# A fused attention, expert and feed-forward kernel: twelve decoding steps change place, and so do the loads of q, k and v

## The chip, the core and the metric

The kernel runs on one core of a Trainium2 chip, as one launch. The metric is the device time of that launch in microseconds; a smaller number is better. Engines are called PE or TensorE (matrix multiply), DVE or VectorE, ACT or ScalarE, POOL or GpSimd, and SP or SyncE, which here only issues DMAs. Every engine works through its own queue in order. Data of the inputs and of intermediate tensors in main memory reach the core's memory by DMA, most of them issued from SP's queue.

## The reference, cut to what matters

```python
def reference(**kwargs):          # q, k, v: 4 batches, 8 heads, 576 positions, 64 wide
    attn_out = _attn_ref(q, k, v) # scores * D, D[i, j] = gamma_h ** (i - j) for i >= j, else 0; times v
    x = attn_out.transpose(0, 2, 1, 3).reshape(B * S, H * D)     # 2304 x 512
    x = _moe_ref(x, ...)          # cosine router, each row to 1 of 8 experts:
                                  # gate * (relu(x @ w1[e]) @ w2[e]), w1 512 x 1024
    return _moe2_ref(x, ...)      # h = x @ w_in; (elu(h)) @ w_out, w_in 512 x 2048
```

## The kernel before, in words

The kernel goes through three stages: attention with the router (line 698 on), the eight experts (line 1247 on), and the last feed-forward part (line 1444 on).

**Attention** is a retention: the decay splits into a factor of the query and one of the key, so that earlier positions can be carried in a small state. It runs over ten units (`UNITS`, line 32). Eight units hold 256 positions of one batch, all heads; two (units 4 and 9) hold the last 64 positions of two batches. In its turn a unit u does, in the order in which the instructions are emitted, and so in the order of each engine's queue:

- `scale(u + 2)` on GpSimd: a copy of q (L289) and a product of k with its decay (L282), each for one tile of a later unit
- `carried(u)`: matmuls of q with the state (L359), then `scores(u, 1)`: matmuls (L334), and a mask on VectorE (L339)
- `transposes(u + 1, 0)`: the scaled q and k of the next unit are transposed on TensorE (L309) and copied out by ScalarE (L317)
- the rows of x of an earlier tile (`xrows`, L427 on TensorE, L439 on VectorE, a store from SP at L448), and `pump`, which emits router steps, small instructions of VectorE, until one needs another engine
- `summed(u + 1)`: the state of the next unit, matmuls of scaled k with v (L396), then additions on VectorE (L403 to L409)
- `transposes(u + 1, 1)`, `values(u)`: matmuls of the masked scores with v (L372), copied out by ScalarE (L378), then `scores(u + 1, 0)`, `xrows`, a second `pump`, and tables for the router on GpSimd (`slots`, L591 to L594)

Between these stand the loads (L261, L264) that SP issues. `load(u, which, behind)` names a unit, one or more of q, k and v, and, where given, a copy of ScalarE that SP waits for before it issues the load. q and k have three buffers, v has four.

**Decoding.** The weights of the last part come as 64-bit numbers. Before they can be used they are turned into 32-bit ones and written to main memory (`wd`), in 32 tiles of 128 x 512. A tile takes four steps (`decode_steps`, line 143), one VectorE instruction each (L151, L153, L156, L159); the second also has a Square on ScalarE (L154), and the fourth issues two DMAs on SP: the load of the tile after next (L137 or L140, 512 KB; there are two buffers) and the store of the finished tile (L161, 256 KB). `decode(n)` emits n steps. `NDECA` (line 698) gives attention units 2 to 6 twelve steps between them, one or two in each `pump`. `decode_load(0)` and `(1)` in unit 1 bring the first two tiles.

**The experts** run through 64 iterations i, eight for each expert: `mm1` (L230, into `h`), then `mm2` of the iteration before (L992 and L994, into `acc`). ScalarE makes hh, the high part of the result of `mm1` (L978), VectorE makes hl, its low part (L979). In each iteration one weight tile is loaded (512 KB) and split into a high part (L199, ScalarE) and a low part (L204, VectorE): w1 in even iterations (ra to ha, la), w2 in odd ones (rb to hb, lb). After the split `decode(2)` emits two steps of decoding (line 1301), through iteration 53. Iterations 9 to 21 also build index tables (`compact`, `compact_part`) on VectorE and GpSimd (L1041). The low part of w2 and hl are read by the matmuls of `mm2`.

The names `u`, `i`, `scale`, `summed`, `load` and `decode` below are these.

Of the kernel before, what the change touches and what calls it, by code (L numbers as in the profile page):

```python
# [14 lines left out]
ALU = mybir.AluOpType  # L15
AX = mybir.AxisListType

P = 128
# [21 lines left out]
NU = len(UNITS)  # L40
# [44 lines left out]
def tile_kernel(ctx: ExitStack, tc: tile.TileContext, q, k, v, emb, tau, w1, w2, w_in, w_out, const, out):  # L85
# [165 lines left out]
    def load(u, which="qkv", behind=None):  # L251
        if u >= NU:
            return
        b, c, _ = UNITS[u]
        r = loaded.setdefault(u, {})
        for nm, src in (("q", q), ("k", k), ("v", v)):
            if nm not in which:
                continue
            t = r[nm] = ld.tile([P, H, 2, D], F32, tag="l" + nm, name=f"{nm}{u}", bufs=4 if nm == "v" else 3)
            if c >= 0:  # L260
                ins = [nc.sync.dma_start(out=t.rearrange("p h s d -> p h (s d)"),  # L261
                                         in_=src[b, :, c * 2 * P:(c + 1) * 2 * P, :].rearrange("h (i s) d -> i h (s d)", s=2))]
            else:
                ins = [nc.sync.dma_start(out=t[64 * j:64 * j + 64, :, 0, :], in_=src[b + j, :, 512:576, :].rearrange("h s d -> s h d"))  # L264
                       for j in range(2)]
            if behind is not None:
                after(ins[0], behind)
# [6 lines left out]
    def scale(u):  # L274
        if u >= NU:
            return
        c = UNITS[u][1]
        scaled[u] = {nm: a2.tile([P, 2, H, D], F32, tag=nm + "s", name=f"{nm}s{u}") for nm in "qk"}
        eng = vec if u == 0 else pool

        def decayed(nm, s_, g_):
            eng.tensor_tensor(out=scaled[u][nm][:, s_], in0=loaded[u][nm][:, :, s_, :],  # L282
                              in1=C("g" + nm)[:, g_ * H:(g_ + 1) * H].unsqueeze(2).to_broadcast([P, H, D]), op=ALU.mult)

        m = len(slots_of(u))
        if u == NU - 1:
            decayed("q", 0, 4)
        else:
            eng.tensor_copy(out=scaled[u]["q"][:, :m].rearrange("p s h d -> p h s d"), in_=loaded[u]["q"][:, :, :m, :])  # L289
        if u == 0:  # L290
            meanwhile()
        for s_ in slots_of(u):
            decayed("k", s_, 2 * c + s_ if c >= 0 else 4)
# [401 lines left out]
            if n == g0 + gn - 1:  # L695
                live.append((gi, interleave(*(then(g(gi), gi, p) for g, p in ((expert_steps, (0, 2)), (gate_steps, (2, NPART)))))))

    NDECA = {2: (1, 1), 3: (1, 1), 4: (1, 1), 5: (1, 1), 6: (2, 2)}
    held = None
    for u in range(NU):  # L700
        ns = UNITS[u][2]
        nd = NDECA.get(u, (0, 0))
        before = UNITS[u - 1][2][1] if u and len(UNITS[u - 1][2]) > 1 else None
        if u:
            scale(u + 2)
            load(u + 3, "q")
        carried(u)
        scores(u, 1 if UNITS[u][1] >= 0 else 0)
        transposes(u + 1, 0, "qk" if u else "k")
        if u == 0:  # L710
            load(2, "k", copied[1, 0, "k"])
            scale(2)
            nc.sync.dma_start(out=ct[:, gcols:], in_=const[:, gcols:CSMALL])
            nc.sync.dma_start(out=big[0][:, 2 * P:], in_=const[:, CSMALL + 2 * P:])
            pool.tensor_scalar(out=pre[:, 0, :], in0=C("base"), scalar1=1.0 / P, scalar2=None, op0=ALU.mult)
            pool.tensor_copy(out=lowb, in_=C("lower"))
            pool.tensor_copy(out=parts[:, :, :2], in_=C("id").rearrange("p (n two) -> p n two", two=2))
        if held is not None:
            grouped(held)
        if before is not None:  # L720
            xrows(before)
        if u < NU - 1:
            pump(24, nd[0])
        summed(u + 1)
        if u == 7:
            load_a(0)
            load_b(0)
            load_a(1)
        transposes(u + 1, 1)
        if u == 0:  # L730
            load(3, "q", copied[1, 1, "k"])
        if u:
            load(u + 3, "k", copied.get((u + 1, 1, "k")))
        if u == 1:
            decode_load(0)
            decode_load(1)
        values(u)
        if u == 0:
            load(3, "k", copied[0, "x"])
        load(u + 2, "v", copied[u, "x"])  # L740
        if before is not None:
            grouped(before)
        if u == NU - 1:
            while live:
                pump(100, 0)
        if u + 1 < NU and UNITS[u + 1][1] >= 0:
            scores(u + 1, 0)
        xrows(ns[0])
        held = ns[0]
        if u < NU - 1:  # L750
            pump(24, nd[1])
        for _ in range(6 if u > 6 else 4):
            if ready:
                slots(*ready.pop(0))
# [492 lines left out]
    for i in range(NI1 + 1):  # L1247
# [46 lines left out]
        if i in (IOVER + 6, IOVER + 7):  # L1294
            next(prep)
            next(prep)
        elif IOVER + 8 <= i < IOVER + 15:
            high(0, i - IOVER - 8)
            low_(0, i - IOVER - 8)
        elif i < IOVER + 6 and i != IOVER - 1:  # L1300
            decode(2)
        if i == NI1 - 3:
            Sa(0)
        if i == NI1 - 2:
# [199 lines left out]
```

## Time and profile before

| | us |
|---|---|
| median of 3 runs (750.96 to 752.85) | 751.32 |
| the profiled execution, whole run | 750.73 |
| the profiled execution, its span | 748.9 |
| TensorE busy | 715.6 (96%) |
| VectorE busy | 587.8 (78%) |
| ScalarE busy | 447.0 (60%) |
| GpSimd busy | 240.8 (32%) |
| moved by DMA | 123.79 MB, mean 165 GB/s |

The span goes from the first to the last instruction that the profiler records; the run is somewhat longer. TensorE is the busiest engine, so the first thing to look for is the stretches where it isn't busy or where its granted clock is below 1.00, and what it waits for there. In the rows below a line of the timeline gives the start and the length in us, the engine, the source line, the instruction, output and inputs, how many of them were merged, and in brackets how long the engine had stood idle before and what ended that.

### The profile page before, as it was taken

The page shows a single profiled execution, that of the slowest core. Times are in us where ns is not written, and L with a number is a line of the kernel's source. Part 1 is how long each engine was busy: PE and PEld are TensorE (multiplying, and loading weights), DVE is VectorE, ACT ScalarE, POOL GpSimd, SP SyncE. Part 2 cuts the span into 40 slices and gives each one's busy share as a digit, 9 for nine tenths or more (in the row PEclk, how much of TensorE's full clock was granted, in tenths as well). Part 3 has the DMA queues.
Part 4 walks back from the last instruction along what each step waited for, and adds up shares of the span by engine and source line. Part 5 has one row for each costly group of instructions (what it writes and reads, how often), then busy time and mean ns, then how long its engine had stood idle before and what let it go on. Part 6 is the DMA issues. An engine that isn't in the chain of part 4 may idle for free.

```text
span 748.9 us, 15511 instructions
## 1 busy us (share of the span) xinstructions
PE 715.6 (96%) x5940; PEld 660.0 (88%) x5940; DVE 587.8 (78%) x940; ACT 447.0 (60%) x690; POOL 240.8 (32%) x347
## 2 busy tenths in 40 slices
PE   7987997999999999989999999999999999999996
PEld 6876984899999999989989998988999998999995
DVE  4458587877887899869789889988778998777773
ACT  3343342555655665656676757777566787666562
POOL 3417236216980240100442133244212227311103
PEclk9999897999999999999999999999999999999999
DMA  7768572788789899888424231234222114221002
GB/s 209 221 206 251 156 227 81 220 283 278 266 288 340 275 291 312 299 310 274 142 85 153 71 99 57 84 114 169 84 61 81 57 58 155 75 80 57 28 29 84
DMA packets 101939, 123.79 MB, mean 165 GB/s; under 512 B 12218, under 2 KB 72030, under 8 KB 101862
## 3 DMA queue, kind: packets, MB, share of 16 engines
q1 hardware_dynamic: 97574, 111.71, 47.1%
q0 software_dynamic: 3104, 9.83, 3.7%
q10 hardware_dynamic: 1184, 1.24, 0.5%
q8 instruction: 47, 0.77, 0.4%
q14 instruction: 30, 0.25, 0.1%
HBM read 99.91 MB, written 22.85 MB: 164 GB/s over the span
## 4 chain that ended last, share of the span: by engine, by line
PE 29%; issue 14%; DVE 7%; POOL 4%; ACT 2%; DMA 2%; SPq 0%; POOLq 0%; ACTq 0%; DVEq 0%
PE o L230 12%; PE X L230 7%; PE Y L230 5%; PE h L230 2%; PE acc L992 2%; DMA draw<-in_moe_w_in_dram 1%; POOL out_dram L1416 1%; PE acc L994 1%; POOL qs L1217 1%; POOL qa L1216 1%; DVE hA L1381 1%; POOL qs L1215 1%; DVE glA L1389 1%; DVE xA L1378 1%; POOL qs L1218 1%
## 5 line engine op out<-in xcount | busy, mean ns | idle before, releaser
L1215 POOL TENSOR_TENSOR qs<-qa 128x256 f32<-128x256 f32 x24 | 23.2, 965 | 250.1 <-DMA qa<-wd 49.7
L230 PE MATMUL h<-xth,ha 128*128 128x332 f32 (+7 forms) x252 | 75.1, 314 | 1.2 <-DVEq L1125 1.2
L992 PE MATMUL acc<-hh,hb 128*128 128x342 f32 (+7 forms) x256 | 73.6, 304 | 2.3 <-ACT hh L978 2.3
L992 PE MATMUL acc<-hh,lb 128*128 128x342 f32 (+7 forms) x256 | 73.5, 303 | 0.3 <-DVE lb L204 0.3
L230 PE MATMUL h<-xtl,ha 128*128 128x332 f32 (+7 forms) x252 | 72.9, 305 | 0.0
L978 ACT ACTIVATE hh<-h 128x342 fp32r<-128x342 f32 (+7 forms) x64 | 27.2, 424 | 46.9 <-PE h L230 44.7
L1368 ACT ACTIVATE rA<-hA 128x768 f32<-128x768 f32 x24 | 20.3, 848 | 55.3 <-DVE hA L1361 55.3
L1353 DVE TENSOR_TENSOR u<-Y,m 128x384 f32<-128x384 f32 x48 | 26.6, 554 | 31.8 <-PE Y L230 29.8
L992 PEld LDWEIGHTS acc<-hh,hb 128*128 128x128 f32 x256 | 48.2, 188 | 2.5 <-ACT hh L978 2.5
L230 PEld LDWEIGHTS h<-xth,ha 128*128 128x128 f32 x252 | 48.0, 191 | 1.7 <-DVEq L1125 1.4
L204 DVE TENSOR_TENSOR la<-ra,ha 128x1024 fp32r<-128x1024 f32 x32 | 39.1, 1222 | 12.5 <-ACT ha L199 12.4
L992 PEld LDWEIGHTS acc<-hh,lb 128*128 128x128 f32 x256 | 48.3, 189 | 0.6 <-DVE lb L204 0.6
L230 PEld LDWEIGHTS h<-xtl,ha 128*128 128x128 f32 x252 | 48.1, 191 | 0.0
L204 DVE TENSOR_TENSOR lb<-rb,hb 128x1024 fp32r<-128x1024 f32 x32 | 39.6, 1236 | 9.7 <-ACT hb L199 9.4
L994 PE MATMUL acc<-hl,hb 128*128 128x342 f32 (+7 forms) x256 | 47.0, 305 | 0.0
L230 PE MATMUL h<-xth,la 128*128 128x332 f32 (+7 forms) x252 | 45.7, 303 | 0.0
L917 POOL DMA_INDIRECT row<-xd,idsp x21 | 21.8, 1038 | 71.4 <-ACT xth L958 68.6
L1416 POOL DMA_INDIRECT out_dram<-ob,idc x18 | 20.3, 1128 | 68.4 <-ACT ob L1413 65.9
L339 DVE TENSOR_TENSOR A<-sc,ctbig 128x512 f32<-128x512 f32 (+1 forms) x36 | 22.0, 653 | 22.7 <-PE sc L334 22.7
L994 PEld LDWEIGHTS acc<-hl,hb 128*128 128x128 f32 x256 | 39.0, 189 | 0.6 <-DVE hl L979 0.3
L317 ACT COPY qT<-qTp 128x512 f32<-128x512 f32 x18 | 11.1, 624 | 47.5 <-PE qTp L309 47.5
L230 PEld LDWEIGHTS h<-xth,la 128*128 128x128 f32 x252 | 38.8, 190 | 0.0
(1690 smaller groups left out, 2342.6 us busy)
## 6 DMA issues: line engine op xcount, KB each, us to landing
ra<-in_moe_w_dram SPq DMA_DIRECT2D x31, 512.0 KB, 5.3
rb<-in_moe_w_dram SPq DMA_DIRECT2D x31, 512.0 KB, 4.7
qb<-wd SPq DMA_DIRECT2D x48, 256.0 KB, 2.8
draw<-in_moe_w_in_dram SPq DMA_DIRECT2D x16, 512.0 KB, 5.7
draw<-in_moe_w_out_dram SPq DMA_DIRECT2D x16, 512.0 KB, 5.3
wd<-db SPq DMA_DIRECT2D x32, 256.0 KB, 5.4
qa<-wd SPq DMA_DIRECT2D x24, 256.0 KB, 2.7
qa<-wd SPq DMA_DIRECT2D x48, 128.0 KB, 2.8
```

Source lines behind the costliest of these rows:

```text
L204: nc.vector.tensor_tensor(out=lo, in0=src, in1=hi.bitcast(F32), op=ALU.subtract)
L230: nc.tensor.matmul(o, l, r, start=first and n_ == 0, stop=last and n_ == len(seq) - 1, skip_group_check=True)
L317: copied[u, s_, nm] = nc.scalar.copy(out=o, in_=pt)
L339: vec.tensor_tensor(out=t[:, :, :w], in0=sc[j][:, :, :w], in1=m.unsqueeze(1).to_broadcast([P, 4, w]), op=ALU.mult)
L917: pool.indirect_dma_start(out=t[:m].rearrange("p k w -> p (k w)"), out_offset=None, in_=xd[:, :], in_offset=bass.IndirectOffsetOnAxis(ap=i ...
L978: nc.scalar.activation(out=hh, in_=hp[:, :c], func=AF.Relu)
L992: nc.tensor.matmul(acc[d][:, :c], w[d][w_], hh, start=f == 0 and w_ == 0, stop=False)
L994: nc.tensor.matmul(acc[d][:, :c], w[d][0], hl, start=False, stop=f == 7)
L1215: pool.tensor_tensor(out=S1, in0=A21, in1=A22, op=ALU.add)
L1353: vec.tensor_tensor(out=S_[nm], in0=S_["Y"], in1=S_["m1"], op=ALU.add)
L1368: nc.scalar.activation(out=Q[n]["r" + z], in_=Q[n]["h" + z], func=AF.Relu, scale=-1.0)
L1416: ins = pool.indirect_dma_start(out=out[:, :], out_offset=bass.IndirectOffsetOnAxis(ap=idc[:, col:col + 1], axis=0), in_=ob, in_offset=None)
```

## The change

In attention:

- The twelve decode steps are gone from attention (`pump(24, 0)`), and the first two decode loads go out in unit 8 instead of unit 1.
- `scale(u + 2)` is emitted after `summed(u + 1)`, not at the unit's start.
- In a unit from 1 on, v of unit u+2 is loaded after the first transposes (it was the last load of the unit), q of unit u+3 after the second transposes (it was the first, at the unit's start), and k of unit u+3 after `values` (it was after the second transposes). Unit 0 and the start of unit 1 load in a matching order.

In the experts, iterations 2 to 13 emit three decode steps instead of two. After iteration 13 as many steps have been emitted as before.

```diff
-    NDECA = {2: (1, 1), 3: (1, 1), 4: (1, 1), 5: (1, 1), 6: (2, 2)}
     for u in range(NU):
-        nd = NDECA.get(u, (0, 0))
-        if u:
-            scale(u + 2)
-            load(u + 3, "q")
+        if u == 1:
+            load(3, "k")
         carried(u)
         scores(u, 1 if UNITS[u][1] >= 0 else 0)
         transposes(u + 1, 0, "qk" if u else "k")
         if u == 0:
             load(2, "k", copied[1, 0, "k"])
-            scale(2)
...
+        else:
+            load(u + 2, "v", copied.get((u + 1, 0, "k")))
...
         if u < NU - 1:
-            pump(24, nd[0])
+            pump(24, 0)
         summed(u + 1)
+        scale(u + 2)
...
         transposes(u + 1, 1)
-        if u == 0:
-            load(3, "q", copied[1, 1, "k"])
-        if u:
-            load(u + 3, "k", copied.get((u + 1, 1, "k")))
-        if u == 1:
+        load(u + 3 if u else 2, "q" if u else "v", copied.get((u + 1, 1, "k")))
+        if u == NU - 2:
             decode_load(0)
             decode_load(1)
         values(u)
-        if u == 0:
-            load(3, "k", copied[0, "x"])
-        load(u + 2, "v", copied[u, "x"])
+        load(u + 3, "k" if u else "q", copied[u, "x"])
...
-            pump(24, nd[1])
+            pump(24, 0)
...
         elif i < IOVER + 6 and i != IOVER - 1:
-            decode(2)
+            decode(3 if 2 <= i < 14 else 2)
```

## Rows read from the trace of the kernel before

**Rows 1.** By stage: stretch, length, PE, PEld, DVE, ACT, POOL busy, clock, DMA share, GB/s
```profile
0.00:138.30 138.30, 115.80 (x2453) 100.27 (x2453) 87.72 (x286) 51.80 (x115) 59.05 (x122) 0.93 0.64 191
138.30:368.00 229.70, 226.14 (x1616) 223.30 (x1617) 191.93 (x289) 137.16 (x232) 74.02 (x98) 0.99 0.87 283
```

**Rows 2.** The same view by attention unit: units 1, 2, 5 and 6
```profile
23.45:35.25 11.80, 10.06 (x258) 9.14 (x257) 5.52 (x13) 4.53 (x10) 4.29 (x7) 1.00 0.65 186
35.25:49.12 13.87, 11.66 (x242) 10.58 (x241) 5.84 (x14) 4.84 (x11) 2.32 (x3) 0.88 0.72 228
...
67.55:83.39 15.84, 12.17 (x234) 10.80 (x232) 9.54 (x12) 3.99 (x8) 6.55 (x13) 0.78 0.44 125
83.39:93.75 10.36, 10.36 (x265) 9.55 (x264) 8.71 (x27) 5.11 (x11) 3.77 (x8) 1.00 0.82 231
```

**Rows 3.** Timeline: the sums of units 1 and 2, and loads before the second
```profile
29.18 1.16 PE L396 MATMUL kv<-v,ks 64*64 64x64 f32 x64 [1.74 <-DMA v<-in_v_dram]
...
33.45 1.16 SPq L137 DMA_DIRECT2D draw<-in_moe_w_in_dram x2
34.72 0.45 SPq L261 DMA_DIRECT2D v<-in_v_dram  x1
...
41.43 1.16 PE L396 MATMUL kv<-v,ks 64*64 64x64 f32 x64 [2.21 <-DMA v<-in_v_dram]
```

**Rows 4.** Timeline: unit 5 up to its sums, and the sums of unit 6
```profile
68.43 1.09 PE L334 MATMUL sc<-qT,kT 64*64 64x128 f32 x28
68.72 4.72 DVE L153 SCALAR_TENSOR_TENSOR db<-draw,db 128x512 int32<-128x512 int32 x1
70.33 2.03 POOL L282 TENSOR_TENSOR ks<-k,ct 128x512 f32<-128x512 f32 x2
73.36 1.28 DVE L339 TENSOR_TENSOR A<-sc,ctbig 128x512 f32<-128x512 f32 x2
74.10 2.57 PE L396 MATMUL kv<-v,ks 64*64 64x64 f32 x64 [3.55 <-DVE A L339]
...
87.31 1.16 PE L396 MATMUL kv<-v,ks 64*64 64x64 f32 x64
```

**Rows 5.** Timeline: k's scaling in units 1 and 4, and transposes that read it
```profile
27.71 2.04 POOL L282 TENSOR_TENSOR ks<-k,ct 128x512 f32<-128x512 f32 x2 [2.20 <-DMA k<-in_k_dram]
...
37.14 0.66 PE L309 MATMUL qTp<-ident,qs 128*128 128x128 f32 x4
...
65.41 2.04 POOL L282 TENSOR_TENSOR ks<-k,ct 128x512 f32<-128x512 f32 x2
...
69.45 0.66 PE L309 MATMUL qTp<-ident,qs 128*128 128x128 f32 x4
```

**Rows 6.** Busy time of two expert stretches; decoding alone (DVE); L153 (ns min/median/max)
```profile
140.27:187.00 46.73, 46.72 (x308) 46.37 (x307) 37.48 (x59) 25.45 (x42) 15.19 (x22) 1.00 0.87 274
...
220.00:240.00 20.00, 20.00 (x151) 19.59 (x150) 17.21 (x27) 11.70 (x20) 3.95 (x4) 1.00 0.95 315
...
140.27:187.00 46.73, 15.38 (x25) 1.00 0.87 274
...
L153 DVE SCALAR_TENSOR_TENSOR db<-draw,db x6: 693/693/695, 141.0 to 179.9; 128x512 int32<-128x512 int32 x6
```

**Rows 7.** Timeline of the expert iterations 8 to 11, four instructions
```profile
170.00 1.23 DVE L204 TENSOR_TENSOR la<-ra,ha 128x1024 fp32r<-128x1024 f32 x1 [2.51 <-ACT ha L199]
...
177.76 0.49 DVE L979 SCALAR_TENSOR_TENSOR hl<-h,hh 128x332 fp32r<-128x332 f32 x1
...
178.30 0.60 PEld L994 LDWEIGHTS acc<-hl,hb 128*128 128x128 f32 x4 [0.28 <-DVE hl L979]
...
181.20 2.09 POOL L1041 TENSOR_SCALAR cb<-ct,posf 128x128 bf16<-128x128 f32 x1
```

**Rows 8.** Decode tiles' loads: issue to landing, from 130 to 200, then 200 to 345
```profile
DMA to landing us min/median/max: 4.6/5.1/6.8
...
DMA to landing us min/median/max: 4.4/5.8/10.0
```

More of the change, by code (lines that the diff above doesn't have):

```diff
@@ L711, in tile_kernel @@
             load(2, "k", copied[1, 0, "k"])
-            scale(2)
             nc.sync.dma_start(out=ct[:, gcols:], in_=const[:, gcols:CSMALL])
             nc.sync.dma_start(out=big[0][:, 2 * P:], in_=const[:, CSMALL + 2 * P:])
-            pool.tensor_scalar(out=pre[:, 0, :], in0=C("base"), scalar1=1.0 / P, scalar2=None, op0=ALU.mult)
-            pool.tensor_copy(out=lowb, in_=C("lower"))
-            pool.tensor_copy(out=parts[:, :, :2], in_=C("id").rearrange("p (n two) -> p n two", two=2))
+        else:
+            load(u + 2, "v", copied.get((u + 1, 0, "k")))
         if held is not None:
@@ L722, in tile_kernel @@
         if u < NU - 1:
-            pump(24, nd[0])
+            pump(24, 0)
         summed(u + 1)
+        scale(u + 2)
+        if u == 0:
+            pool.tensor_scalar(out=pre[:, 0, :], in0=C("base"), scalar1=1.0 / P, scalar2=None, op0=ALU.mult)
+            pool.tensor_copy(out=lowb, in_=C("lower"))
+            pool.tensor_copy(out=parts[:, :, :2], in_=C("id").rearrange("p (n two) -> p n two", two=2))
         if u == 7:
```

## The prediction

> **What bounds the kernel now.** I read the busy time by stage first [rows 1]. In the experts TensorE is busy 226.14 of 229.70 us. In the head, attention and routing, it is busy 115.80 of 138.30 us, at a mean granted clock of 0.93 of full speed. What the change does to the time has to come from TensorE's gaps in attention, or from new gaps in the experts.
>
> Then the same table by attention unit [rows 2]; a unit's border is where its first `carried` matmul starts. Unit 6 (83.39 to 93.75) is filled by TensorE and takes 10.36 us. Unit 1 takes 11.80, unit 2 takes 13.87 and unit 5 takes 15.84 us. Units 2 and 5 also have a granted clock of 0.88 and 0.78: part of them ran at 1.2 instead of 2.4 GHz. So these three carry the loss, and the timeline says why.
>
> Units 1 and 2: TensorE stands before the sums (L396) for 1.74 and 2.21 us until v lands [rows 3]. The second of these loads was issued at 34.72, at the end of the unit before, behind two decode loads (33.45) in SP's queue, and took 6.7 us.
>
> Unit 5: the scores end at 69.52 and VectorE should mask them at once. But it is inside a decode step (L153) that began at 68.72 and took 4.72 us, while GpSimd scaled k and worked at tables [rows 4]. The mask comes at 73.36 and the sums at 74.10, after 3.55 us of idle TensorE, and they take 2.57 us, where the same 64 matmuls took 1.16 in unit 6. A stall is therefore paid twice, as idle time and as a stretch at 1.2 GHz behind it.
>
> **The change part by part.** The terms are taken from the profiled execution: span 748.9, run 750.73 us, which is 0.59 below the median of 751.32.
>
> *v goes out earlier.* In unit u the load of v for u+2 now follows the first k copy of u+1; it was behind the unit's last copy. (In unit 0 it follows the second k copy.) So v has most of a unit more to land, and needs 6 to 7 us [rows 3]. Unit 1 loses its wait, 1.7 us. Unit 2 loses 2.21 us and the slow clock behind it: from the sums to the next unit it took 49.12 - 41.43 = 7.69 us, unit 6 took 93.75 - 87.31 = 6.44 [rows 2 to 4], so 1.25 more. Sum: 1.7 + 3.5 = 5.2 us.
>
> *Decode steps leave attention.* Twelve steps are three tiles of four VectorE steps (L151, L153, L156, L159), and each tile has one Square on ScalarE and one load and one store on SP besides. Unit 5: without L153 the mask pair could run from 69.5 to 70.8 (1.28 us), so the sums start 3.2 us sooner; from the sums to the next unit it took 83.39 - 74.10 = 9.29 us against 6.44, so 2.85 more. Together 6.0 us. In the other units the steps lie beside TensorE and I count nothing for them. The Squares hide behind ScalarE's waits in either place.
>
> *k's scaling follows the sums; q and k go out later.* `scale(u+2)` moves on GpSimd from the start of a unit to about its middle, 4 to 5 us. In unit 1 it ended at 29.75 and TensorE transposed that tile in unit 2 at 37.14: 7.4 us to spare, so about 2.5 are left [rows 5]. In unit 4 it ran from 65.41 to 67.45, at the unit's end, because tables emitted before it fill GpSimd's queue; the transposes came at 69.45, 2.0 us later, and there the new place changes nothing. SP waits for a copy at three places of a unit as before. Behind those waits stand the x rows' stores, which nothing reads before routing, and the next loads. Cost taken: 0; without that cover up to 2 us a unit.
>
> *The first two decode loads* move from unit 1 to unit 8: 1 MB that no one needs before the experts. GpSimd's constants only move behind `scale(2)`. Cost: 0.
>
> *Twelve expert iterations decode three steps instead of two*, those between 140.27 and 187.00. VectorE is busy 37.48 of 46.73 us there, and a step costs 15.38 / 25 = 0.62 us on average [rows 6]. The twelve come to 7.4 us, so VectorE would be 96% full. Whether TensorE waits is a question of order. VectorE runs late by 0.62 us more each iteration until it meets a wait for ScalarE, where it is on time again; the last such wait is the 2.51 us before 170.00 [rows 7]. After it VectorE also makes the index tables, and the hl that it begins at 177.76 already holds up TensorE today, by 0.28 us at 178.30. Two added steps (iterations 8 and 9) stand between and go straight onto TensorE, 1.24 us; of the next iteration's 0.62 I count all. So 1.9 us. The bounds are 0 (all of it fits into 9.25 us of idle time) and 7.4 (all of it on TensorE's path).
>
> DMA in that stretch: 3 x 768 KB more in 46.7 us is 50 GB/s on 274. From 220 to 240 the chip moved 315 GB/s with TensorE busy 20.00 of 20.00 us [rows 6], close to the 324 that this makes. Cost to the weights: 0. From iteration 14 on as many steps are done as before, and all that follows is the same.
>
> *A rule against the change.* What the row shows: beside GpSimd's work L153 took 4.72 us, where it takes 0.69 in the experts [rows 4, 6]. The Trainium skill (SBUF — State Buffer, "Who interferes with whom") says that a VectorE instruction with two SBUF inputs and a GpSimd instruction that reads SBUF exclude each other, and that whichever issues first keeps the port for the whole instruction. By that rule L153 should have waited for one GpSimd instruction (1.02 us of k's scaling) and not for a series; the trace agrees in kind and not in size. By the rule the moved steps meet the same in iterations 9 to 13, where GpSimd builds tables, with the price of rival E.
>
> In those iterations the rows show the other side giving way: a table instruction takes 2.09 us at 181.20 [rows 7], and no L153 of the stretch takes over 0.695 [rows 6].
>
> **Sum:** 750.73 - 1.7 - 3.5 - 6.0 + 1.9 = 741.4; with 0.59 to the median, **742.0 us**. Attention gives 11.2 us, the experts take 1.9.
>
> **The rivals.**
> *A: the next wait takes the place.* The early v and the missing L153 give back the idle times alone (1.74 + 2.21 + 3.2 = 7.2 us), but something small (router steps on VectorE, a copy) fills the rest: 751.3 - 7.2 + 1.9 = 746.0. For it: other small waits of TensorE must remain between units of 10 us. Against it: unit 6 has the same work and no gap.
> *B: the later scaling becomes the bound.* If k lands so late for its scaling that TensorE waits 2 us in each of five units, 10 us go: 751.3 - 11.2 + 10 + 1.9 = 752.0. For it: GpSimd already waits 2.20 us for k in unit 1 [rows 5]. Against it: 7.4 us were to spare, and three decode tiles of 768 KB less move in attention.
> *C: the extra steps cost their whole length:* 751.3 - 11.2 + 7.4 = 747.5. For it: the hl that is late already. Against it: the wait of 2.51 us.
> *D: slower, by decode loads that come late.* With two buffers a load is issued five steps before its first use. At three steps in an iteration of 3.9 us that is 6.5 us; landing took 4.6, 5.1 and 6.8 us (least, median, most) in that stretch [rows 8]. If it takes L, an iteration can't be shorter than 0.6 L, for VectorE and ScalarE both stand there, and TensorE follows: 12 x (0.6 L - 3.9). From L = 8.1 us on this outweighs the 11.2 us. At 10.0 us, the most seen later, it is 25.2 us and the time 765.3. Against it: the median of 5.1.
> *E: the port.* Tables hold five moved steps (iterations 9 to 13) for 1.04 us each, 5.2 us more on VectorE with no wait there to hide it: 751.3 - 11.2 + 1.9 + 5.2 = 747.2. The row at 181.20 speaks against it.
>
> **How the numbers follow.** Chances: forecast 0.62 (own range 739 to 745), A 0.14, B 0.07, C 0.05, D 0.08, E 0.04. The range runs from 738.5 (nothing lost in the experts, 740.1, and units 1, 2 and 5 half a microsecond better than unit 6) to 748.5, which takes in A, C and E and leaves out B and D. About 0.3% of 751.3, 2.3 us, is what a measurement here can tell from no change; faster is below 749.0. Forecast, A, C and E make 0.85, less 0.01 for their edges; B with that edge is the same, and D slower: 0.84, 0.08, 0.08.
>
> **What would show it.** Right: units 1, 2 and 5 of 10 to 10.6 us at granted clock 1.00; no wait of L396 for v; the first expert matmul some 11 us earlier; the twelve iterations about 2 us longer than 46.7, with waits for hl or lb around the index tables; all behind them as long as before. Wrong: transposes (L309) that wait for GpSimd (B), VectorE or ScalarE that wait for the decode tile in iterations 3 to 13 (D), table work that runs on past the matmuls that read it, or a unit still at 0.8.

## The result, and the profile after

The changed kernel takes 742.27 us (median of 4 runs, 741.50 to 745.80); the kernel before, beside it, took 752.09 (4 runs, 750.96 to 753.31). The ratio is 0.9878, with a 95% interval of 0.9841 to 0.9916. A later series of 12 runs gave 743.37 (738.95 to 748.91) against 750.35, ratio 0.9905 (0.9870 to 0.9939). The profiled run took 741.50 us with a span of 739.7 (before 750.73 and 748.9). Every ratio in this document leaves out the runs that lie over 1.5% above the fastest of the same kernel; of the 31 runs of the kernel before that head the table of the experiments six are left out, and the median of the other 25 is 748.80.

The time is what was predicted. The way to it is not: attention gave more than its sum, the experts took more than theirs, so that the two misses nearly cancel, and one of the terms in attention has another cause than the prediction gave it.

The same view of the attention units 1, 2, 5 and 6 as in [rows 2], then the routing stretch (end of unit 8 to the first expert matmul) and the experts' first 22 iterations, 0 to 21 (columns as in [rows 1]):

```profile
23.38:33.37 9.99, 9.99 (x258) 9.12 (x257) 5.48 (x13) 4.53 (x10) 3.39 (x5) 1.00 0.84 242
33.37:43.34 9.97, 9.97 (x241) 9.10 (x241) 5.43 (x13) 4.51 (x10) 1.65 (x2) 1.00 0.55 154
61.66:71.06 9.40, 9.31 (x235) 8.28 (x233) 4.40 (x10) 3.90 (x8) 5.81 (x12) 1.00 0.72 201
71.06:81.20 10.14, 10.14 (x264) 9.37 (x263) 6.68 (x24) 4.51 (x10) 3.51 (x8) 1.00 0.65 188
...
100.04:119.86 19.82, 13.34 (x196) 9.12 (x196) 16.23 (x74) 6.29 (x15) 12.86 (x34) 0.83 0.36 113
119.86:206.65 86.79, 83.71 (x548) 81.54 (x549) 71.53 (x111) 49.08 (x81) 47.55 (x66) 1.00 0.90 286
```

And the last two stretches of the kernel before:

```profile
112.67:133.89 21.22, 14.49 (x197) 9.64 (x196) 16.25 (x74) 6.17 (x15) 12.96 (x34) 0.76 0.23 73
...
133.89:216.69 82.80, 82.45 (x549) 81.53 (x549) 65.62 (x100) 47.42 (x78) 45.16 (x64) 1.00 0.86 277
```

Units 1, 2 and 5, which took 11.80, 13.87 and 15.84 us, now take 9.99, 9.97 and 9.40 at full clock. Routing takes 1.40 us less, with the clock at 0.83 where it was 0.76. The first expert matmul begins 14.03 us earlier. The 22 expert iterations take 3.99 us more; there TensorE is idle for 3.08 us, where it was idle for 0.35.

The sums of units 1 and 2 have lost their wait for v, and in unit 5 nothing stands before the sums (timeline, TensorE and GpSimd, as in [rows 3, 4]):

```profile
27.29 1.16 PE L396 MATMUL kv<-v,ks 64*64 64x64 f32 x64
...
37.27 1.16 PE L396 MATMUL kv<-v,ks 64*64 64x64 f32 x64
...
62.54 1.09 PE L334 MATMUL sc<-qT,kT 64*64 64x128 f32 x28
63.55 0.66 PE L309 MATMUL qTp<-ident,qs 128*128 128x128 f32 x4
64.05 0.60 PE L309 MATMUL kTp<-ident,ks 128*128 128x128 f32 x4
64.58 1.57 PE L396 MATMUL kv<-v,ks 64*64 64x64 f32 x64
...
64.91 2.03 POOL L282 TENSOR_TENSOR ks<-k,ct 128x512 f32<-128x512 f32 x2
```

In the experts the loss sits where iteration 10 passes into 12, and again between 14 and 16. The timeline of the first of these, with the decode tile's load on SP's queue:

```profile
158.96 0.42 SPq L140 DMA_DIRECT2D draw<-in_moe_w_out_dram  x1
...
162.96 1.22 DVE L204 TENSOR_TENSOR lb<-rb,hb 128x1024 fp32r<-128x1024 f32 x1
164.09 0.70 DVE L153 SCALAR_TENSOR_TENSOR db<-draw,db 128x512 int32<-128x512 int32 x1
164.83 0.74 DVE L156 SCALAR_TENSOR_TENSOR db<-draw,db 128x512 int32<-128x512 int32 x1
165.68 0.69 DVE L159 SCALAR_TENSOR_TENSOR db<-dsq,db 128x512 f32<-128x512 f32 x1
166.29 0.50 DVE L974 SCALAR_TENSOR_TENSOR hl<-h,hh 128x332 fp32r<-128x332 f32 x1
...
165.29 0.66 ACT L154 ACTIVATE dsq<-draw 128x512 f32<-128x512 f32 x1 [4.40 <-DMA draw<-in_moe_w_out_dram]
165.85 0.44 ACT L973 ACTIVATE hh<-h 128x332 fp32r<-128x332 f32 x1
...
164.23 0.42 PE L987 MATMUL acc<-hh,lb 128*128 128x332 f32 x1 [0.88 <-DVE lb L204]
...
166.84 0.88 PE L989 MATMUL acc<-hl,hb 128*128 128x332 f32 x4 [1.27 <-DVE hl L974]
```

(L973, L974, L987 and L989 are the L978, L979, L992 and L994 of before.) TensorE waits for lb and then for hl, as predicted: three decode steps stand ahead of hl on VectorE. But the second wait has a second cause. ScalarE stood for 4.40 us before the Square of a decode tile whose load had gone out at 158.96, and hh, which hl needs, is queued behind that Square.

### The profile page after: what moved, and what is told of

Its sections match the earlier page's. It is cut to its first block, busy times and chain, and to the rows that moved or that the text cites. A ratio compares the mean times of both kernels' runs of the same rounds, so it can differ in the third digit from the quotient of the medians.

```text
span 739.7 us, 15521 instructions
## 1 busy us (share of the span) xinstructions
PE 710.7 (96%) x5939; PEld 655.6 (89%) x5940; DVE 585.1 (79%) x940; ACT 446.9 (60%) x690; POOL 241.9 (33%) x347
## 3 DMA queue, kind: packets, MB, share of 16 engines
q10 hardware_dynamic: 1184, 1.24, 0.5%
## 4 chain that ended last, share of the span: by engine, by line
PE 29%; issue 14%; DVE 7%; POOL 4%; ACT 2%; DMA 2%; SPq 0%; POOLq 0%; ACTq 0%; DVEq 0%
PE o L230 12%; PE X L230 7%; PE Y L230 5%; PE h L230 2%; PE acc L987 2%; DMA draw<-in_moe_w_in_dram 2%; POOL out_dram L1411 1%; PE acc L989 1%; POOL qs L1212 1%; POOL qs L1213 1%; POOL qa L1211 1%; DVE hA L1376 1%; POOL qs L1210 1%; DVE glA L1384 1%; DVE xA L1373 1%
## 5 line engine op out<-in xcount | busy, mean ns | idle before, releaser
L987 PE MATMUL acc<-hh,hb 128*128 128x342 f32 (+7 forms) x256 | 74.2, 306 | 3.5 <-ACT hh L973 3.5
L987 PE MATMUL acc<-hh,lb 128*128 128x342 f32 (+7 forms) x256 | 74.3, 306 | 1.1 <-DVE lb L204 1.1
L987 PEld LDWEIGHTS acc<-hh,hb 128*128 128x128 f32 x256 | 48.6, 190 | 3.7 <-ACT hh L973 3.7
L987 PEld LDWEIGHTS acc<-hh,lb 128*128 128x128 f32 x256 | 48.8, 191 | 1.7 <-DVE lb L204 1.7
L989 PE MATMUL acc<-hl,hb 128*128 128x342 f32 (+7 forms) x256 | 47.5, 308 | 1.9 <-DVE hl L974 1.9
L973 ACT ACTIVATE hh<-h 128x342 fp32r<-128x342 f32 (+7 forms) x64 | 27.1, 424 | 36.4 <-PE h L230 36.1
L912 POOL DMA_INDIRECT row<-xd,idsp x21 | 22.8, 1087 | 71.4 <-ACT xth L953 68.4
L989 PEld LDWEIGHTS acc<-hl,hb 128*128 128x128 f32 x256 | 39.3, 191 | 3.3 <-DVE hl L974 3.2
L339 DVE TENSOR_TENSOR A<-sc,ctbig 128x512 f32<-128x512 f32 (+1 forms) x36 | 22.1, 654 | 21.5 <-PE sc L334 21.5
L154 ACT ACTIVATE dsq<-draw 128x512 f32<-128x512 f32 x32 | 21.7, 677 | 26.1 <-DMA draw<-in_moe_w_in_dram 14.1
```

The lines of the kernel that those rows point to most:

```text
L154: nc.scalar.activation(out=sq, in_=hw.bitcast(F32), func=AF.Square)
L339: vec.tensor_tensor(out=t[:, :, :w], in0=sc[j][:, :, :w], in1=m.unsqueeze(1).to_broadcast([P, 4, w]), op=ALU.mult)
L912: pool.indirect_dma_start(out=t[:m].rearrange("p k w -> p (k w)"), out_offset=None, in_=xd[:, :], in_offset=bass.IndirectOffsetOnAxis(ap=i ...
L973: nc.scalar.activation(out=hh, in_=hp[:, :c], func=AF.Relu)
L987: nc.tensor.matmul(acc[d][:, :c], w[d][w_], hh, start=f == 0 and w_ == 0, stop=False)
L989: nc.tensor.matmul(acc[d][:, :c], w[d][0], hl, start=False, stop=f == 7)
```

## The experiments

Every trace was read in the same way: a unit begins at its first `carried` matmul, the experts at the first matmul into `h`. All numbers are us; a ratio is to the kernel before in the same series. The lead of a trace is how much earlier it begins an iteration than the trace of the kernel before.

| kernel | unit 1 | unit 2 | unit 4 | unit 5 | unit 7 | experts begin | 22 iterations | median (runs) | ratio to before |
|---|---|---|---|---|---|---|---|---|---|
| before | 11.80 | 13.87 | 10.52 | 15.84 | 11.06 | 133.89 | 82.80 | 750.5 (31) | |
| changed | 9.99 | 9.97 | 10.40 | 9.40 | 10.98 | 119.86 | 86.79 | 742.27 (4) | 0.9878 |
| changed, second trace | 9.99 | 9.97 | 10.41 | 9.40 | 10.99 | 120.69 | 89.88 | 743.37 (12) | 0.9905 |
| order alone | 9.99 | 9.97 | 11.20 | 9.40 | 14.04 | 125.55 | 82.81 | 741.78 (10) | 0.9906 |
| decoding alone | 11.72 | 10.58 | 15.27 | 10.25 | 10.63 | 127.79 | 87.44 | 750.96 (10) | 1.0030 |
| changed, scaling early | 9.99 | 9.97 | 15.00 | 9.40 | 10.99 | 125.12 | 89.30 | 747.83 (10) | 0.9962 |
| one step later | 11.90 | 12.80 | 10.29 | 9.80 | 11.18 | 127.98 | 82.81 | 751.28 (10) | 1.0019 |
| v alone | 11.65 | 9.97 | 10.29 | 9.40 | 11.10 | 125.42 | 82.80 | 745.19 (10) | 0.9936 |
| eight and four | 9.99 | 9.97 | 11.19 | 9.40 | 10.63 | 121.43 | 83.41 | 740.24 (6) | 0.9864 |
| steps in the last part | 9.99 | 9.97 | 10.40 | 9.40 | 10.99 | 120.77 | 82.73 | 740.93 (6) | 0.9870 |

### The two halves of the change, each by itself

The order of loads and scaling as changed, the decode steps where they were (`NDECA` and `decode(2)` of before, the first two decode loads in unit 1):

```diff
+    NDECA = {2: (1, 1), 3: (1, 1), 4: (1, 1), 5: (1, 1), 6: (2, 2)}
...
-            decode(3 if 2 <= i < 14 else 2)
+            decode(2)
```

> The changed order of loads and of scaling, with the twelve decode steps left in attention. Theory: v's late load makes the waits of units 1 and 2, a decode step makes that of unit 5. Then units 1 and 2 take 10.0 to 10.4 us as in the changed kernel, unit 5 stays near 15.8, the experts stay as before; 746 us (752 less 1.8 and 3.9). Rival: the decode loads' traffic and their place ahead of v in SP's queue make the wait; then unit 2 stays above 12 us and the time is 749 or more.

The decode steps as changed, the order of loads and scaling as before:

```diff
-    NDECA = {2: (1, 1), 3: (1, 1), 4: (1, 1), 5: (1, 1), 6: (2, 2)}
+    NDECA = {}
...
-            decode(2)
+            decode(3 if 2 <= i < 14 else 2)
```

> The decode steps moved as in the change, the order of loads and scaling as before. Theory: unit 5 falls to about 9.4 us (6.4 less), unit 1 stays at 11.8, unit 2 loses about 1.2 us because no decode load stands ahead of v; the experts lose 4.9 us as in the changed kernel, and routing is 1.4 us shorter; 748 us. Rival (traffic): units 1 and 2 fall to 10 us too, and the time comes to 743 as with the whole change.

The order alone gives 741.78 us (739.31 to 745.24), ratio 0.9906 (0.9868 to 0.9945): all that the whole change gives. Moving the decode steps alone gives nothing: 750.96, ratio 1.0030 (0.9989 to 1.0071). Both miss the theory of the prediction. Decoding alone says one thing of v as well: with no decode loads ahead of it in SP's queue, v came only 0.54 us late in unit 2 (10.58 us for 13.87), although its load was as late as before. So in this pair of traces most of that wait goes with those two loads, which the prediction names; unit 1 keeps its own (1.67 us).

The traces say why. With the order alone unit 5 is 9.40 us although its L153 is still there (timeline, VectorE, GpSimd and TensorE):

```profile
64.45 0.83 DVE L153 SCALAR_TENSOR_TENSOR db<-draw,db 128x512 int32<-128x512 int32 x1
65.28 1.29 DVE L339 TENSOR_TENSOR A<-sc,ctbig 128x512 f32<-128x512 f32 x2
66.49 1.25 DVE L156 SCALAR_TENSOR_TENSOR db<-draw,db 128x512 int32<-128x512 int32 x1
...
64.95 1.26 POOL L594 TENSOR_TENSOR At<-o,parts 128x48 bf16<-128x48 bf16 x4
66.15 1.03 POOL L289 COPY qs<-q 128x1024 f32<-128x1024 f32 x1
67.15 2.49 POOL L282 TENSOR_TENSOR ks<-k,ct 128x512 f32<-128x512 f32 x2
...
66.21 1.57 PE L396 MATMUL kv<-v,ks 64*64 64x64 f32 x64
```

L153 takes 0.83 us in place of 4.72. It starts half a microsecond before the last tables (L594) and is done when the copy of q begins. In the kernel before it started in the midst of those tables, and lasted through the copy and the products of [rows 4] as well (timeline of before, GpSimd):

```profile
68.33 1.05 POOL L594 TENSOR_TENSOR At<-o,parts 128x48 bf16<-128x48 bf16 x4
69.33 1.03 POOL L289 COPY qs<-q 128x1024 f32<-128x1024 f32 x1
```

A start in the midst of the tables is not enough, though. The kernel of the experiment on VectorE's time, below, has the attention of the kernel before, instruction for instruction. In its trace L153 starts amid the same tables and is let through (timeline, VectorE and GpSimd):

```profile
71.71 0.70 DVE L153 SCALAR_TENSOR_TENSOR db<-draw,db 128x512 int32<-128x512 int32 x1
...
71.02 1.57 POOL L594 TENSOR_TENSOR At<-o,parts 128x48 bf16<-128x48 bf16 x4
```

(Unit 5 took 12.57 us there, but by other waits.) So the 4.72 us belong to one execution of this attention and not to each. What decides between the two is not shown.

With the decode steps gone and the old order, unit 5 takes 10.25 us, but unit 4 takes 15.27 us. What stands there is no decode step (timeline, VectorE and GpSimd):

```profile
60.11 3.19 DVE L581 TENSOR_TENSOR gate<-gate,parts 128x5 f32<-128x5 f32 x1
...
63.58 0.22 DVE L581 TENSOR_TENSOR gate<-gate,parts 128x5 f32<-128x5 f32 x1
...
60.23 1.03 POOL L289 COPY qs<-q 128x1024 f32<-128x1024 f32 x1
61.23 2.03 POOL L282 TENSOR_TENSOR ks<-k,ct 128x512 f32<-128x512 f32 x2
```

L581 works on 128 x 5 elements and takes 0.22 us at 63.58; at 60.11 it is held until GpSimd's copy and two products are done. So the stall is a meeting of GpSimd's series with whichever VectorE instruction comes at or shortly before the start of the scaling. It needs no decode step.

The order alone has one long unit of its own, unit 7 with 14.04 us. There a decode step is held beside the scaling, and the mask behind it comes late (timeline, VectorE and GpSimd):

```profile
85.89 1.53 DVE L159 SCALAR_TENSOR_TENSOR db<-dsq,db 128x512 f32<-128x512 f32 x1
...
84.38 1.48 POOL L282 TENSOR_TENSOR qs<-q,ct 128x512 f32<-128x512 f32 x1 [0.31 <-DMA q<-in_q_dram]
85.83 1.04 POOL L282 TENSOR_TENSOR ks<-k,ct 128x512 f32<-128x512 f32 x1
```

### What sets the meeting: the place of the scaling

The changed kernel with the scaling back at the start of each unit:

```diff
+        if u:
+            scale(u + 2)
         carried(u)
...
         summed(u + 1)
-        scale(u + 2)
         if u == 0:
+            scale(2)
```

> The changed kernel with the scaling back at the start of each unit; loads and decode steps as in the changed kernel. Theory 1 (what matters is when GpSimd's series meets VectorE, which the scaling's place sets): a VectorE instruction of over 2 us is back in units 3 to 7 of the profile, or times spread again by over 6 us, and the median is 744 to 748. Theory 2 (the earlier v is what counts in attention, scaling has no part, as the prediction costs it at 0): 741.5 to 743.

It takes 747.83 us (745.89 to 749.12), theory 1. All units are as in the changed kernel but unit 4, 15.00 us against 10.40, with the same held L581, and the clock falls to 0.89 (by unit; then the timeline):

```profile
51.52:66.52 15.00, 10.30 (x235) 8.82 (x233) 10.98 (x31) 4.20 (x11) 12.38 (x24) 0.89 0.72 211
...
57.99 3.19 DVE L581 TENSOR_TENSOR gate<-gate,parts 128x5 f32<-128x5 f32 x1
...
62.35 2.41 PE L334 MATMUL sc<-qT,kT 64*64 64x128 f32 x32 [4.08 <-DVE S L403]
```

So the step that the prediction priced at 0, and B even at a loss, is worth 15.00 - 10.40 = 4.6 us in this trace and about 4.3 in the ratios (0.9962 - 0.9905 = 0.0057 of 750).

All traces together say the same. Of the six with the scaling at the unit's start (before, decoding alone, scaling early, one step later, v alone, VectorE's time) four have a VectorE instruction of 2.97 to 4.72 us between unit 1 and the end of unit 8. Of the seven with the scaling after the sums none has one over 1.53 us.

The counter-test leaves GpSimd's scaling out. It is the kernel before, decode steps and order as they were; from unit 4 on the transposes and sums take the scaled tiles of unit 3, so the scaling of later units is left out:

```diff
         c = UNITS[u][1]
+        if u > 3:
+            scaled[u] = scaled[3]
+            return
```

> The kernel before, but from unit 4 on the transposes and sums take the scaled q and k of unit 3 (the scaling and copying of five units is left out), so GpSimd has only its table instructions there; the decode steps stay in attention. Theory 1: the 4.72 us of L153 is a meeting of whichever VectorE instruction is at hand with GpSimd's series of tables and scaling (without decode steps it met L581, 3.19 us, in the other order of scaling L156, 2.97 us). Then no VectorE instruction of units 4 to 7 takes over 1.5 us, unit 5 takes 9.4 to 10.4 us, the median falls by 4 to 7 us to 744 to 746, and the runs lie closer together than the 14 us of the kernel before (742 to 756). Theory 2, of the prediction: it belongs to the decode step; then L153 still takes over 3 us in unit 5 and the time stays at 750.

Only its attention can be read: the rows then go to other experts and the whole takes 861.28 us, so the time expected of it was a miss of the design. In attention theory 1 holds. GpSimd has nothing to do in unit 5, L153 takes 0.68 us, the L156 from unit 1 to unit 7 take the same, and unit 5 takes 9.40 us at full clock (by unit; timeline; then VectorE's groups from 24 to 105):

```profile
67.54:76.94 9.40, 9.36 (x235) 8.31 (x233) 5.59 (x12) 3.88 (x8) 0.00 (x0) 1.00 0.70 194
...
68.70 0.68 DVE L153 SCALAR_TENSOR_TENSOR db<-draw,db 128x512 int32<-128x512 int32 x1
69.53 1.29 DVE L342 TENSOR_TENSOR A<-sc,ctbig 128x512 f32<-128x512 f32 x2 [0.15 <-PE sc L337]
...
L156 DVE SCALAR_TENSOR_TENSOR db<-draw,db 128x512 int32<-128x512 int32 x3 | 2.0, 682 | 0.0
```

L153 begins 1.16 us into unit 5, as it did in the kernel before (1.17). What is gone beside it is GpSimd's work, the tables as well as the scaling, since these were done earlier.

### Moving one step, and v by itself

One decode step of unit 5 half a unit later in the kernel before:

```diff
-    NDECA = {2: (1, 1), 3: (1, 1), 4: (1, 1), 5: (1, 1), 6: (2, 2)}
+    NDECA = {2: (1, 1), 3: (1, 1), 4: (1, 1), 5: (0, 2), 6: (2, 2)}
```

> The kernel before with one decode step of unit 5 (L153, 4.72 us long) emitted half a unit later, after the sums. Theory: the step costs what it does because it meets GpSimd's work at that place and stands ahead of the mask; unit 5 falls from 15.8 to 9.5 to 10.5 us, all else as before; 746 us. Rival: any place in units 4 to 6 meets GpSimd's work, the step is as long elsewhere and the stall only moves; 750 to 752 us.

Only the load of v earlier, from unit 1 on:

```diff
+        if u:
+            load(u + 2, "v", copied.get((u + 1, 0, "k")))
...
-        load(u + 2, "v", copied[u, "x"])
+        if u == 0:
+            load(2, "v", copied[0, "x"])
```

> The kernel before with v's load alone moved to its new place from unit 1 on; q, k and scaling stay. Theory: v is all that counts in the new order, so unit 2 falls to about 10 us as with the whole order, unit 1 stays at 11.8 (its v is loaded in unit 0, which is unchanged); 748 us. Rival: v's earlier load only pushes q's and k's back, the scaling comes late and the transposes wait; unit 2 stays above 12 us.

One step moved: 751.28 us, ratio 1.0019 (0.9975 to 1.0063), the time that the rival gives. Its trace has unit 5 at 9.80, but that run took 747.08 and is the second fastest of ten: one profile showed the stall gone, eight of the ten runs were slower than it. Where those eight lose their time no trace shows.

v alone: 745.19, ratio 0.9936 (0.9896 to 0.9976), better than the theory's 748. Unit 2 is 9.97, as the prediction had it, unit 1 keeps its wait since its load is not moved here. The runs stand in three groups: 740.5 to 741.5 (three), 744.2 to 745.3 (three), 749.4 to 750.0 (four). The steps between them, 4 and 5 us, are about the price of one meeting; that they are meetings is not shown, since only one of these runs has a trace. It is of the fastest: unit 5 at 9.40, although its L156 was held for 2.97 us, at a place where TensorE did not need the engine. This trace, too, has L153 and the old place of the scaling, and no stall of TensorE in unit 5. So a program whose scaling lies on the edge of a meeting can have it in some executions and not in others, as the kernel before does (4.72 and 0.70 us for the same L153). With the new place of the scaling the two traces of the changed kernel agree within 0.01 us in every unit of the table. The changed kernel's times still spread by 10 us (738.95 to 748.91); what the two traces show of that lies mostly in the experts.

### What the third decode step costs in the experts

VectorE's time by itself, in the kernel before, without loads, Squares or stores:

```diff
             decode(2)
+            if 2 <= i < 14:
+                vec.tensor_tensor(out=idle, in0=idle, in1=idle, op=ALU.mult)
```

> The kernel before with one more VectorE instruction on a 128x512 tile of its own (about 0.7 us, as long as a decode step) in each of the iterations 2 to 13, and no load, no Square and no store with it. Of the changed kernel the lead shrank by 4.06 us from iteration 2 to 22. Theory 1: that comes from ScalarE, which stands before a Square for a decode tile that is still on its way (4.40 us before 165.29); then these instructions alone cost at most 1.9 us, the prediction's own sum, and the time is 751 to 752.5. Theory 2: it is VectorE's time by itself; then the iterations 2 to 22 lose 3.5 to 5 us and the time is 754 to 755.

The changed kernel without the loads of decode tiles 2 to 13 (they take the words of tiles 0 and 1 again, so the words of tiles 2 to 13 are missing from the output):

```diff
     def decode_load(i):
...
+        if 2 <= i < 14:
+            drw[i] = kept[i % 2]
+            return
```

> The changed kernel with the loads of decode tiles 2 to 13 left out (they take the words of tiles 0 and 1 again), all VectorE steps, Squares and stores as they were. Theory 1 (ScalarE waits for the loads): the lead over the kernel before shrinks from iteration 2 to 22 by 0 to 1.9 us in place of 4.06, no Square waits for a load in iterations 3 to 13, and the time is 738.5 to 740.5. Theory 2 (VectorE's time): it shrinks by 3.5 to 4.5 us as before, 742. Theory 3 (the stores): VectorE still waits over 3 us for them in all and the lead shrinks by over 3 us.

Theory 1 of both, that ScalarE's wait for the loads is the cause, falls. Without the loads the 22 iterations still take 86.43 us (82.80 before, 86.79 and 89.88 in the two traces of the changed kernel), and the time is 743.75. With VectorE's time alone they take 89.66, and the time is 757.56, ratio 1.0093 (1.0048 to 1.0137), even more than theory 2 expected. (The traces are of runs of 747.17 and 759.79 us, both above their medians.) In the trace with VectorE's time alone nothing is lost up to iteration 11 (the experts begin at 136.37 there, though attention is the program of before); 1.22 us are lost between 11 and 12, and 5.67 between 20 and 22. What happens there (timeline, GpSimd, ScalarE and TensorE):

```profile
211.95 0.73 POOL L1043 TENSOR_TENSOR ca<-co,parts 128x90 bf16<-128x90 bf16 x1
212.83 1.06 POOL L917 DMA_INDIRECT row<-xd,idsp  x1 [0.16 <-issue]
...
219.43 0.72 ACT L928 ACTIVATE row<-row,gslp 128x512 f32<-128x512 f32 x1 [7.83 <-DMA row<-xd,idsp]
...
220.20 0.42 PEld L953 LDWEIGHTS tp<-ident,row 128*128 128x128 f32 x4 [4.17 <-ACT row L928]
```

GpSimd gathers the rows of the next expert (L917), and the gather is queued behind its index tables (L1041 to L1043). In the kernel before, it went out at 204.39, 9.25 us after iteration 16 began. There the gather waited for TensorE and not for the tables. Here it went out 14.02 us after iteration 16 began, right behind the tables, which ran late. A little of that is a late start: counted from the beginning of iteration 9 the tables begin after 9.41 us, in the kernel before after 8.80. Most of it is their length: the 36 table instructions ahead of the gather took 31.98 us in place of 26.34, stretched where they meet VectorE. The rows landed late, ScalarE stood 7.83 us before weighting them (with hb behind it in its queue) and TensorE stood 4.17 before transposing them.

### The same kernel again, and other places for the twelve steps

> The changed kernel once more, for a second trace of the same program and beside the three that follow. If the stalls of attention depend on how the engines happen to meet, the traces of one program differ: then units 1, 2 and 5 stay under 10.5 us here (v's early load is no matter of meeting) while units 4, 6 or 7 may differ by some us. Median 742.3, between 740 and 746.

The second trace of the changed kernel has the same attention, and another loss in the experts: 7.08 us in place of 3.99. Just before iteration 21 (timeline):

```profile
196.38 2.11 POOL L912 DMA_INDIRECT row<-xd,idsp  x1 [0.15 <-issue]
...
204.83 0.72 ACT L923 ACTIVATE row<-row,gslp 128x512 f32<-128x512 f32 x1 [6.98 <-DMA row<-xd,idsp]
...
205.61 0.66 PE L948 MATMUL tp<-ident,row 128*128 128x128 f32 x4 [3.07 <-ACT row L923]
```

(L912, L923 and L948 are L917, L928 and L953 of before.) The gather goes out 11.31 us after iteration 16 began; in the first trace it was 9.27, and little was lost there. The 36 table instructions ahead of it took 29.48 us, 27.91 in the first trace. The expectation had looked for differences in attention; there were none.

The third steps in every other iteration from 2 to 24:

```diff
-            decode(3 if 2 <= i < 14 else 2)
+            decode(3 if 2 <= i < 26 and i % 2 == 0 else 2)
```

> The changed kernel with the twelve third steps in every other iteration from 2 to 24, not in each from 2 to 13. Theory (VectorE falls behind by up to three steps in a row until the two decode buffers run empty): spread out they cost 1 to 2 us in the experts in place of 4.9, time 738.5 to 740. Rival (each step past the second costs its turn wherever it stands): 742 to 743.

743.76 us, ratio 0.9910 (0.9879 to 0.9940): the rival. It loses 0.6 us up to iteration 20 and 3.1 between 20 and 21, again before the gathered rows, then 0.9 up to 23 and 1.4 between 26 and 27, where a Square waits 2.63 us for its tile. Spreading the steps out did not help; half of them still lie beside GpSimd's tables, which took 29.27 us ahead of the gather.

No third step in the experts, twelve in the last part:

```diff
-            decode(3 if 2 <= i < 14 else 2)
+            decode(2)
...
-        if n < 5:
+        if n < 6:
-                ex[f"E{j}"] = ex.get(f"E{j}", []) + [lambda: decode(1)]
+                ex[f"E{j}"] = ex.get(f"E{j}", []) + [lambda n=n: decode(2 if n < 5 else 1)]
```

> The changed kernel with two decode steps in each early expert iteration, as before the change, and the twelve that are then missing done two at a time in the last part. Theory: attention keeps its 14.1 us, the experts lose at most 1 us against the kernel before, and VectorE's slack in the last part takes half of 12 x 0.62 us: 737.5 to 740. Rival: the last part has no slack on VectorE, the whole 7.4 us and the loads' waits come onto its path: 744 to 748.

The order alone, with the four steps of unit 6 in iterations 2, 4, 6 and 8:

```diff
-    NDECA = {2: (1, 1), 3: (1, 1), 4: (1, 1), 5: (1, 1), 6: (2, 2)}
+    NDECA = {2: (1, 1), 3: (1, 1), 4: (1, 1), 5: (1, 1)}
...
-            decode(2)
+            decode(3 if i in (2, 4, 6, 8) else 2)
```

> The changed kernel's order of loads and scaling; the eight decode steps of units 2 to 5 stay in attention, the four of unit 6 go to iterations 2, 4, 6 and 8. With all twelve in attention unit 7 took 14.04 us (10.98 without), behind a decode step of 1.53 us, and nothing was lost in the experts. Theory: unit 7 is 11 us again and the experts lose under 1 us: 738.5 to 740. Rival: another VectorE instruction meets GpSimd's series in another unit, and the time is that of the order alone, 741.5 to 743.

Steps in the last part: 740.93 us (739.38 to 742.07), ratio 0.9870 (0.9824 to 0.9916), slightly above the theory. The experts take 82.73 us for 22 iterations, nothing lost; 12.8 us of lead at iteration 63 shrink to 748.9 - 740.0 = 8.9 at the end, so the twelve steps cost 3.9 us there. Eight and four: 740.24 us (738.39 to 741.65), ratio 0.9864 (0.9817 to 0.9911), also slightly above its range, with a trace of 736.6. Unit 7 is 10.63 where the order alone had 14.04, and the experts lose 0.61. The medians are 2.4 and 3.1 us below the changed kernel's in the same series; the intervals overlap, so that they beat it is likely and not shown. The table work ahead of the gather is that of the kernel before in both traces (26.33 us).

## Why the prediction was right, and where its steps were not

**v earlier: right.** Units 1 and 2 give 1.81 and 3.90 us for 1.7 and 3.5. Unit 2 falls to the same 9.97 where v alone goes earlier. The predicted look is there: no wait of L396 for v. The sizes hold for this pair of traces: with v's load at its old place and the decode loads ahead of it, unit 2 took 11.75 to 13.99 us in four traces.

**Decode steps leave attention: the size was right and the cause was wrong.** Unit 5 gives 15.84 - 9.40 = 6.44 us for a predicted 6.0, but not because L153 left. With L153 in place and the new order it gives the same 6.44; without GpSimd's scaling it does, too; without L153 and with the old scaling the stall returns in unit 4 on L581. That the size came out is partly luck: the row was that of an execution with the stall, and in another execution of the same attention L153 took 0.70 us. The step that failed is "without L153 the mask pair could run from 69.5": the row named the instruction that was held, and I took it for the cause. What the decode steps do cost in attention shows in the order alone, in unit 7: 14.04 us against 10.98. It was not there in the kernel before (11.06).

**The scaling follows the sums: priced at 0, in fact a gain of the size of v's.** Put back alone in the changed kernel, it costs 4.6 us. I asked only whether its results come in time. They do: GpSimd waits for k up to 3.02 us, and among TensorE's waits of 0.2 us and more in the changed kernel's attention there is none for GpSimd. I did not ask whom it meets on the way. Rival B, its loss, did not come. Nor did rival A: units 1, 2 and 5 take under 10 us, and nothing fills the gaps.

The instructions held longest in attention are L153, L156, L159, L472, L474 and L581, whose two inputs are tiles that engines or loads leave in SBUF. L409, with one input from the matmuls' sums, took 0.42 us at 59.03 in the changed kernel, while GpSimd's copy of q began at 58.99. That agrees with the Trainium skill (SBUF — State Buffer, "Who interferes with whom"), by which a VectorE instruction with two SBUF inputs contends with GpSimd's reads, and one with at most one SBUF input, outside the modes that use two ports, does not. The page's lock for one whole instruction does not explain the length: L581 was held through three GpSimd instructions in a row (a copy and two products, 60.23 to 63.26).

**Experts: the term that was mis-sized.** 1.9 us was forecast, with 0 and 7.4 as bounds; the two traces show 3.99 and 7.08. The two steps that go "straight onto TensorE, 1.24 us" are there: VectorE's time alone lost 1.22 us between iterations 11 and 12. Two paths were not in the sum. The first is ScalarE's, where the prediction has the Squares "hide": a Square that waits for its tile holds hh up (4.40 us at 165.29). That is the mechanism of rival D, and its sign came: ScalarE waited for a decode tile four times in the first 22 iterations, 11.1 us in all. But TensorE lost much at one of these places only, not in every iteration; the 2.4 us lost there are made of this and of VectorE's order, since without the loads 1.4 remain. The second contradicts "all that follows is the same": VectorE's third steps make GpSimd's tables start later and take longer; the gather is queued behind them, and its delay comes back just before iteration 21. That is the waiting table work named as a sign of being wrong, but by way of a gather and not of the matmuls that read the tables. The loads are not needed for the loss: without them 3.63 us go, with VectorE's time alone 6.86. How the 3.99 and 7.08 us divide between the two paths stays open. Rival C's 7.4 is near what the second trace shows. Rival E had the meeting right and the loser wrong: from iteration 2 to 22 no decode step took over 0.83 us in either trace, and the tables were the ones that grew.

**The stores.** I named the loads as what could come late and not the store of the finished tile (`wd`), whose buffers are also two; VectorE waited 4.3 us for it in three places of the changed kernel's first trace. Without the decode loads VectorE did not wait for a store at all and 3.63 us were lost all the same, so theory 3 of that experiment falls. What the stores' waits cost beside the loads was not tried by itself.

**Why the sum came out.** Attention and routing gave 14.0 us up to the first expert matmul for 11.2 predicted; 1.4 of the 2.8 more is in routing, which the change does not touch and which took 19.8 to 21.5 us in the traces, at granted clocks from 0.75 to 0.92. The experts took 4.0 for 1.9 by iteration 22, and 0.9 more by the end, in iterations 52 to 56, where the lead of different traces grows or shrinks by up to 3.5 us; that part is not settled. The misses nearly cancel: 748.9 - 739.7 = 9.2 in the profiles, 9.3 predicted. That the forecast of 742.0 came within half a microsecond is luck. The prediction also took 2.3 us as what a measurement can tell from no change; single runs of the changed kernel lie up to 10 us apart.

**Where the gain is.** The order of loads and scaling has all of it. Moving the decode steps takes 3.1 us out of unit 7 and 0.8 out of unit 4, and puts 4 to 7 into the experts; with the order changed, it brings nothing that these runs can tell from 0 (741.78 without it, 742.27 and 743.37 with it). Within the order, v's early load from unit 1 on has 745.19 of the same series, and 741.78 is 3.4 us less; how much of these is the scaling and how much unit 1's v, no run separates.

## What to carry to other kernels

When one engine's instruction is many times longer than its fellows, look at what the other engine does in that time before you blame or move the instruction; ask also what else would stand in its place, since the stall stays with the series that causes it. A step that only shifts work on an engine off the critical path is to be priced by whom it will meet, not only by whether its result is in time. And where runs of one program spread by 10 us, a single profile shows one of several executions; a term read from it needs a second trace or an experiment.

## What the runs showed of the hardware

- A VectorE instruction with two inputs in SBUF that begins just before or within a series of GpSimd instructions can be held through several of them: 3.19 us for 128 x 5 elements (0.22 otherwise), 4.72 for a decode step (0.68 with GpSimd idle at the same moment). It need not be: the same step amid the same tables took 0.70 in another trace.
- It goes the other way too: beside decode steps GpSimd's pair of products took 2.49 us, not 2.03, and in the experts of the changed kernel's first trace one index-table instruction (L1037) took 1.69 us at 202.87, beside a split and a decode step, and 0.33 at 201.56, with VectorE idle.
- Whether the meeting happens changes between executions of the same instructions (the 4.72 and 0.70 us above are one step of one attention program). v alone had run times in three groups 4 to 5 us apart, which would fit it.
